# Transposes that read 104 of 128 partitions, loads by head padded to 48 rows, and new offsets in a planner's list

## The chip, the cores and the metric

The kernel runs on one core of one Trainium2 chip. The metric is the device time of one execution in microseconds (us). Three runs of the kernel before gave 744.09, 746.27 and 746.48 us, a median of 746.27. Inside the core, five engines work from queues of their own, each strictly in the order of its queue: TensorE (PE in the profile; its weight loads are shown apart as PEld), VectorE (DVE), ScalarE (ACT), GpSimd (POOL) and SyncE (SP). POOL and SP issue the DMAs here.

## What is computed

The kernel has two stages that follow one another. The first is a recurrence over 768 time steps for 4 batches x 8 heads with a 40 x 40 state each; the second is a two-layer network on the 3072 rows that the first stage gives:

```python
for t in range(S):                                   # S = 768, D = 40, 32 (batch, head) pairs
    y[:, :, t] = np.einsum('bhd,bhde->bhe', rt, state)
    Sa = np.einsum('bhde,bhe->bhd', state, at)
    state_decay = state * wt[:, :, None, :] - np.einsum('bhd,bhe->bhde', Sa, bt)
    state = state_decay + np.einsum('bhd,bhe->bhde', vt, kt)
...
h = x @ w_in                                         # 3072 x 320 times 320 x 2048
sp = np.where(h > 20.0, h, np.log1p(np.exp(np.minimum(h, 20.0))))
g = h * np.tanh(sp)
return (g @ w_out).astype(np.float32)                # times 2048 x 320
```

## The kernel before, in words

**Chunks.** The 768 steps are cut into 12 chunks (`c`) of 64 steps. Inside a chunk the recurrence is solved as a triangular system, so that it becomes matrix products. The 32 (batch, head) pairs are split three ways: `be` (two halves, for which most tiles exist twice), `al` (two halves that lie on partitions 0 to 39 and 64 to 103 of one tile; partitions 40 to 63 and 104 to 127 carry nothing), and 8 along the free dimension, which the steps take in two groups `g` of 4.

**Stages of a chunk.** `pre_a` (lines 316 to 413) prepares a chunk's half: loads `wa` (line 322) and `bk` (line 325), two scans on DVE (343, 348), products on PE (386) whose results ACT and DVE pick up (389 to 394), and transposes of `bk` on PE (410), copied by ACT (412). `inv` (415 to 479) inverts the 32 x 32 triangles of two chunks at once: a DVE transpose (420), then thirty rounds of a multiply (425) and an add (428), each of which needs the one before it, and two DVE transposes (430 into `TT`, 432 into `GP`). There are six such inverses. PE combines their results (444, 452) and forms `KT` (476). Then come the steps of the chunk, which carry the state `ST` from chunk to chunk: `step_a` (PE 514, ACT 517), `step_b` (PE 557, DVE 560), `step_u` (PE transposes 528, ACT 530), `step_d` (PE transposes 544 of the state, ACT 546 into `smd`), `step_c` (PE 586 and 591, DVE 596 and 602 make the new state, ACT 598 the output). `step_loads` (484 to 495) brings in the next chunk's `VS`, `UVT` and `bdr` from POOL's queue; `UVT` and `bdr` exist once, so the load of `bdr` for a chunk waits for the last line 591 of the chunk before it.

**The network.** Its weights are split into two parts of fewer bits by DVE and ACT (`convert`, lines 716 to 740: 12 pieces of `w_in` and 8 of `w_out`; DVE's part is lines 733, 734, 736 and 739). `load_x` (774 to 798) brings the recurrence's output back and splits it likewise (DVE 792, 794, 796; ACT 793). `mlp1` (PE 814, ACT 817 and 818, DVE 819) and `mlp2` (PE 835 to 837) make 48 units of work in a fixed chain.

**What sets the order.** No queue's order is written by hand. The code records its operations in a `Plan` with what each reads and writes, an estimated duration, and buffers drawn from pools; `Plan.order` (129 to 204) then places them one by one. Of the operations that could start on an engine within a look-ahead of the earliest, it takes the one with the highest priority: the length of the work that hangs on it plus an offset from `PRIO`, a table with one number for each kind of operation and chunk (`sa0` is `step_a` of group 0, and so on). The look-ahead is the constant `LOOK` plus an entry of the table `LOOKS`, which is empty before. So a change of these numbers, or of an operation's estimated duration, can move any instruction.

## Time and profile before

| what | before |
|---|---|
| median of three runs | 746.27 us |
| the profiled execution, its own time | 745.79 us |
| its span, first to last instruction | 744.0 us |
| PE busy / DVE busy / ACT busy / POOL busy | 678.6 / 456.0 / 420.8 / 102.2 us |
| first matmul of the network (line 814) starts | 393.74 us |
| moved by DMA | 61.81 MB, mean 83 GB/s |

Times inside the profile count from the span's start. A row of a table by line gives line, engine, operation, output and inputs, shapes, number of instructions, then the busy time, the mean duration of one in ns and the idle time in front of them with what ended it. In the chain of waits a row has start, duration and what stood there; in a table of stretches each engine has its busy time and, in brackets, the number of instructions, then come the granted TensorE clock, the DMA share and GB/s. A matmul in 32-bit floats counts as two instructions of PE, a transpose as one. The ends of matmuls are modelled, so that PE's busy time overstates how full it is; the pace of back-to-back matmuls (from the chain of waits) is the better measure.

### The profile page before, as it was taken

What the parts mean: (1) busy time and instruction counts of PE and PEld (TensorE: products, weight loads), DVE (VectorE), ACT (ScalarE), POOL (GpSimd) and SP (SyncE); (2) the same over time, 40 slices, a digit from 0 to 9 for tenths busy, and PEclk for the clock granted to TensorE, in tenths of its full rate; (3) what the DMA queues carried; (4) which work ended last, traced back from release to release, by engine and by line L of the source; (5) the groups of instructions that cost most, each with busy time, mean ns of one, the idle gap of its engine ahead of it and who ended that gap; (6) DMA issues with size and microseconds to landing.
All of it is one profiled execution on the core that took longest, in us unless ns stands there. A gap on an engine that the chain in (4) does not pass through costs nothing.

```text
span 744.0 us, 17243 instructions
## 1 busy us (share of the span) xinstructions
PE 678.6 (91%) x7048; PEld 626.0 (84%) x7048; DVE 456.0 (61%) x975; ACT 420.8 (57%) x937; POOL 102.2 (14%) x166
## 2 busy tenths in 40 slices
PE   2554698999999999999989999999999999999997
PEld 1544698998999989999978999898998989999897
DVE  7999999899999999999368853123113113111110
ACT  4554576867887787888858644234334324323332
POOL 9111013142224223212220000000000000000000
PEclk9778589999999999999999999999999999999999
DMA  7533214364444445144587713003004001000100
GB/s 191 171 98 89 64 39 104 77 139 116 107 109 111 101 118 150 37 117 128 123 220 185 206 46 100 0 12 97 14 1 103 18 1 40 19 0 1 36 1 35
DMA packets 58206, 61.81 MB, mean 83 GB/s; under 512 B 25536, under 2 KB 48704, under 8 KB 58128
## 3 DMA queue, kind: packets, MB, share of 16 engines
q1 hardware_dynamic: 49296, 40.94, 19.6%
q0 software_dynamic: 8832, 19.79, 10.8%
q8 instruction: 55, 0.90, 0.5%
q14 instruction: 23, 0.19, 0.1%
HBM read 48.79 MB, written 11.86 MB: 82 GB/s over the span
## 4 chain that ended last, share of the span: by engine, by line
PE 64%; DVE 22%; ACT 7%; issue 4%; DMA 1%; POOL 0%; ACTq 0%; DVEq 0%
PE ps L814 24%; PE ps L835 7%; PE ps L837 7%; PE ps L836 7%; PE ps L557 4%; DVE XL L428 3%; DVE tmp L425 3%; PE ps L386 3%; PE ps L586 3%; DVE P L343 2%; DVE bk L354 2%; PE ps L476 2%; PE ps L528 2%; DVE HA L394 2%; PE ps L591 1%
## 5 line engine op out<-in xcount | busy, mean ns | idle before, releaser
L819 DVE TENSOR_TENSOR gl<-g,gh 128x1024 fp32r<-128x1024 f32 x48 | 58.8, 1225 | 194.9 <-ACT gh L818 188.7
L817 ACT ACTIVATE g<-ps 128x512 f32<-128x512 f32 x96 | 57.0, 597 | 173.6 <-PE ps L814 173.3
L837 PE MATMUL ps<-w_oh,gl 128*128 128x320 f32 x384 | 118.6, 309 | 0.0
L835 PE MATMUL ps<-w_oh,gh 128*128 128x320 f32 x384 | 118.5, 309 | 0.0
L836 PE MATMUL ps<-w_ol,gh 128*128 128x320 f32 x384 | 118.5, 309 | 0.0
L814 PE MATMUL ps<-xh,w_ih 128*128 128x512 f32 x288 | 113.2, 393 | 0.0
L814 PE MATMUL ps<-xh,w_il 128*128 128x512 f32 x288 | 97.7, 393 | 0.0
L386 PE MATMUL ps<-bk,ad 128*128 128x168 f32 x384 | 68.7, 340 | 26.9 <-DVE bk L354 18.2
L386 PEld LDWEIGHTS ps<-bk,ad 128*128 128x128 f32 x384 | 63.8, 215 | 28.8 <-issue 26.5
L814 PE MATMUL ps<-xl,w_ih 128*128 128x512 f32 x192 | 75.4, 393 | 0.0
L836 PEld LDWEIGHTS ps<-w_ol,gh 128*128 128x128 f32 x384 | 72.1, 188 | 2.1
L835 PEld LDWEIGHTS ps<-w_oh,gh 128*128 128x128 f32 x384 | 72.1, 188 | 2.0
L837 PEld LDWEIGHTS ps<-w_oh,gl 128*128 128x128 f32 x384 | 72.1, 188 | 0.0
L814 PEld LDWEIGHTS ps<-xh,w_il 128*128 128x128 f32 x288 | 54.1, 188 | 12.3
L814 PEld LDWEIGHTS ps<-xh,w_ih 128*128 128x128 f32 x288 | 54.2, 188 | 10.6 <-issue 0.2
L428 DVE TENSOR_TENSOR XL<-XL,tmp 128x30 f32<-128x30 f32 (+9 forms) x180 | 58.7, 326 | 2.0
L425 DVE TENSOR_TENSOR tmp<-XL 128x30 f32<-128x30 f32 (+9 forms) x180 | 58.5, 325 | 1.7
L557 PE MATMUL ps<-bdr,UVT 128*128 128x128 f32 x384 | 48.8, 283 | 4.9 <-ACT UVT L517 2.7
L818 ACT CAST gh<-g 128x1024 fp32r<-128x1024 f32 x48 | 50.4, 1050 | 1.5
L557 PEld LDWEIGHTS ps<-bdr,UVT 128*128 128x128 f32 x384 | 46.1, 197 | 6.0 <-ACT UVT L517 3.4
L476 PE MATMUL ps<-bdT,HA 128*104 128x128 f32 x384 | 46.9, 280 | 2.4 <-ACT bdT L468 2.4
L476 PEld LDWEIGHTS ps<-bdT,HA 128*104 128x104 f32 x384 | 44.1, 174 | 4.1 <-ACT bdT L468 2.2
(89 smaller groups left out, 1170.9 us busy)
## 6 DMA issues: line engine op xcount, KB each, us to landing
wa<-in_wa SPq DMA_DIRECT2D x48, 162.5 KB
bk<-in_bk SPq DMA_DIRECT2D x48, 160.0 KB
cv<-in_wi SPq DMA_DIRECT2D x12, 512.0 KB
cv<-in_wo SPq DMA_DIRECT2D x8, 640.0 KB
pD<-P POOLq DMA_DIRECT2D x48, 81.2 KB, 2.5
bdr<-in_rD POOLq DMA_DIRECT2D x24, 160.0 KB, 4.5
UVT<-in_vD POOLq DMA_DIRECT2D x24, 160.0 KB, 4.0
VS<-in_vN POOLq DMA_DIRECT2D x24, 160.0 KB, 4.7
```

The lines of the kernel that those rows point to most:

```text
L386: PE.matmul(pv()[:, j], ad[:, s0 + j].rearrange("p k a t -> p (k a t)"), bk[:, s0 + j], start=(j == 0), stop=True, skip_group_check=True)
L425: op('V', (0.16 + m * i * 0.00104), lambda tv=tv, i=i, m=m: V.tensor_tensor(out=tv, in0=X[:, i + 1:32, i:i + 1].broadcast_to([128, m, i]), ...
L428: op('V', (0.16 + m * i * 0.00104), lambda tv=tv, i=i: V.tensor_tensor(out=X[:, i + 1:32, 0:i], in0=X[:, i + 1:32, 0:i], in1=tv, op=ALU.ad ...
L476: PE.matmul(kv()[:, j], ha.t[:, s0 + j], bd[:, o + s0 + j].rearrange("p a t -> p (a t)"), start=(j == 0), stop=True, skip_group_check=True)
L557: PE.matmul(qv()[:, s], UVT[:, g * 4 + s, be * 128:be * 128 + 128], bdr[:, be, g * 4 + s].rearrange("p a t -> p (a t)"), start=(s == 0), s ...
L814: PE.matmul(b.t, w, x, start=(n == 0), stop=(n == 7), skip_group_check=True)
L817: op('A', 0.6, lambda b=b, j=j: A.activation(g.t[:, j], b.t, AF.Mish), r=[b], w=[(g, j)])
L818: op('A', 1.05, lambda: A.copy(gh.t, g.t), r=[(g, 0), (g, 1)], w=[gh])
L819: op('V', 1.226, lambda: V.tensor_tensor(out=gl.t, in0=g.t, in1=gh.t.bitcast(F32), op=ALU.subtract), r=[(g, 0), (g, 1), gh], w=[gl])
L835: PE.matmul(o, gh.t[:, j, t], oh, start=(f == 0 and j == 0), stop=False, skip_group_check=True)
L836: PE.matmul(o, gh.t[:, j, t], ol, start=False, stop=False, skip_group_check=True)
L837: PE.matmul(o, gl.t[:, j, t], oh, start=False, stop=(f == 7 and j == 1), skip_group_check=True)
```

## The change

Four things are changed.

1. The three kinds of transposes on PE (lines 410, 528, 544) read partitions 0 to 103 of their input and multiply by a 104 x 104 part of the identity. So each gives 104 columns instead of 128, and four of them lie at a distance of 104 in PSUM. A helper `heads` picks the two times 40 wanted columns out of each. The copy of line 546 now takes only these 320 columns a partition (512 before), into an `smd` of 344 columns, and the matmul of line 591 takes its 64 weight columns from there at a distance of 40.
2. The loads of `wa`, `bk`, `UVT` and `bdr` bring 48 rows to each half's partitions instead of 40. The host pads the arrays with zeros (ones for the decay). So the partitions 40 to 47 and 104 to 111 are written by each load.
3. The planner's estimates for these operations are changed (for a group of four transposes 0.44 to 0.357, for the copy of line 546 0.58 to 0.43, lower figures for the loads).
4. `PRIO` has other numbers in every row, and `LOOKS` gets 21 rows.

```diff
+LOOKS = {
+    'zero': (0, 0, 0, 0, 0, 0.5, 0,),
...
 PRIO = {
-    'zero': (-99, -65, 338, 745, 81, -91, -72.5, 60, -47.5, -354, -210, 224.5,),
+    'zero': (-646.5, -1464.5, -1517.5, -811, -977, -824, -689, -662, -634.5, -1290, -1244, -1362,),
...
+    used = slice(0, 104)
+    rows = cst[used, 0:104]
+    heads = lambda x: bass.AP(x.tensor, x.offset, [x.ap[0], [104, 4], [64, 2], [1, 40]])
...
-    newSMD = make(wk, 2, [128, 4, 128], "smd")
+    newSMD = make(wk, 2, [128, 344], "smd")
...
+    op('G', 0.2, lambda: [G.memset(t[:, 320:344], 0.0) for t in S.smd], w=['smd0'])
...
-            q = slice(al * 64, al * 64 + 40)
-            op('S', 0.45, lambda q=q, al=al: SP.dma_start(out=wa[q], in_=I['wa'][c, be, al]), w=[('wz', be, al), ('a', be, al)], lat=1.95, srv=1.0)
+            q = slice(al * 64, al * 64 + 48)
+            op('S', 0.45, lambda q=q, al=al: SP.dma_start(out=wa[q], in_=I['wa'][c, be, al]), w=[('wz', be, al), ('a', be, al)], lat=1.95, srv=0.76)
...
-                    PE.transpose(pv()[:, j].rearrange("p a b -> p (a b)"), bk[:, s0 + j, xo:xo + 128], ident)
-            op('P', 0.44, tr, r=BK + ['cst', 'bkn0'], w=[b], mode=128, work=0.42, claim=[bkn])
+                    PE.transpose(pv()[:, j], bk[used, s0 + j, xo:xo + 128], rows)
+            op('P', 0.357, tr, r=BK + ['cst', 'bkn0'], w=[b], mode=128, work=0.347, claim=[bkn])
...
-                    PE.transpose(tv()[:, s].rearrange("p a d -> p (a d)"), UVT[:, g * 4 + s, be * 128:be * 128 + 128], ident)
+                    PE.transpose(tv()[:, s], UVT[used, g * 4 + s, be * 128:be * 128 + 128], rows)
...
-                PE.transpose(dv()[:, s], st[:, 2 * s:2 * s + 2].rearrange("p a d -> p (a d)"), ident)
-        op('P', 0.44, tr, r=[('ST', g), 'cst'], w=[b], mode=128, work=0.42)
-        op('A', 0.58, lambda: A.copy(smd.t, dv()), r=[b], w=[smd])
+                PE.transpose(dv()[:, s], st[used, 2 * s:2 * s + 2].rearrange("p a d -> p (a d)"), rows)
+        op('P', 0.357, tr, r=[('ST', g), 'cst'], w=[b], mode=128, work=0.347)
+        op('A', 0.43, lambda: A.copy(smd.t[:, 0:320].rearrange("p (s a d) -> p s a d", a=2, d=40), heads(b.t)), r=[b, 'smd0'], w=[smd])
...
-                            PE.matmul(py[be * 64:be * 64 + 64, 2 * j:2 * j + 2, 0:64], smd.t[:, s0 + j, be * 64:be * 64 + 64],
+                            PE.matmul(py[be * 64:be * 64 + 64, 2 * j:2 * j + 2, 0:64], smd.t[:, (s0 + j) * 80 + be * 40:(s0 + j) * 80 + be * 40 + 64],
```

The lines of the changed kernel are 28 higher than those of the kernel before, from the loads on. The number of matmuls, DVE and ACT operations and DMAs is the same; where they stand is not. Three places show it.

DVE, before, inside the sixth and last inverse (lines 425 and 428 are its rounds, 430 the transpose that ends them; 560, 596, 602 and 571 belong to the steps of a chunk, `cv` and `w_il` to the conversion of the network's weights):

```order
L739 SCALAR_TENSOR_TENSOR w_il_3855<-cv_3859,w_ih_3854 128x512
L425 TENSOR_TENSOR tmp<-XL 128x220
L596 TENSOR_TENSOR stn_135<-ST_115,ps_68 128x160
L428 TENSOR_TENSOR XL<-XL,tmp 128x11x20
L596 TENSOR_TENSOR stn_135<-ST_115,ps_63 128x160
L425 TENSOR_TENSOR tmp<-XL 128x210
L602 TENSOR_TENSOR ST_115<-stn_135,R_134 128x8x40
L428 TENSOR_TENSOR XL<-XL,tmp 128x10x21
L596 TENSOR_TENSOR stn_136<-ST_116,ps_65 128x160
L425 TENSOR_TENSOR tmp<-XL 128x198
L571 TENSOR_TENSOR R_134<-rw_130,rw_131 128x8
L428 TENSOR_TENSOR XL<-XL,tmp 128x9x22
```

DVE, changed, from the end of the same inverse (458 is 430 before, 624 is 596, 630 is 602, 599 is 571, 762 and 767 are 734 and 739):

```order
L458 STREAM_TRANSPOSE TT<-XL 128x32x32
L624 TENSOR_TENSOR stn_135<-ST_115,ps_66 128x160
L460 STREAM_TRANSPOSE GP_149<-TT 64x32x32
L624 TENSOR_TENSOR stn_135<-ST_115,ps_69 128x160
L624 TENSOR_TENSOR stn_136<-ST_116,ps_63 128x160
L630 TENSOR_TENSOR ST_115<-stn_135,R_133 128x8x40
L624 TENSOR_TENSOR stn_136<-ST_116,ps_64 128x160
L599 TENSOR_TENSOR R_133<-rw_130,rw_131 128x8
L630 TENSOR_TENSOR ST_116<-stn_136,R_134 128x8x40
L599 TENSOR_TENSOR R_134<-rw_130,rw_131 128x8
L762 SCALAR_TENSOR_TENSOR cv_3983<-cv_3983 128x512
L767 SCALAR_TENSOR_TENSOR w_il_3977<-cv_73,w_ih_3976 128x512
```

The state update of one chunk (two of line 602 with what leads to them) and part of the weights' conversion stood ahead of the end of the inverse and stand behind it now. Counted over the whole queue ahead of the sixth line 430: four of line 596, two each of 571, 602, 733, 734 and 736 and three of 739 fewer than before. A round of the inverse (425 or 428) that follows another with nothing between them is found 108 times in the six inverses before, and 80 times in the changed queue (31 and 43 of these in the sixth).

PE, before, ahead of the first use of the sixth inverse (line 444 reads `TT`; 528 and 557 are transposes and products of the ninth chunk, counted from 0):

```order
L528 MATMUL ps_67<-cst,UVT 128x128 x4
L557 MATMUL ps_68<-bdr,UVT 128x128 x4
L557 MATMUL ps_63<-bdr,UVT 128x128 x4
L528 MATMUL ps_64<-cst,UVT 128x128 x4
L528 MATMUL ps_65<-cst,UVT 128x128 x4
L444 MATMUL ps_66<-TT,GP_149 32x32 x32
```

PE, changed, behind the first use of the sixth inverse (472 is 444 before, 542 is 514, 572 is 544, 556 is 528, 585 is 557):

```order
L472 MATMUL ps_65<-TT,GP_149 32x32 x32
L542 MATMUL ps_62<-KT_127,VS_109 64x64 x8
L542 MATMUL ps_62<-KT_128,VS_110 64x64 x8
L542 MATMUL ps_66<-KT_127,VS_109 64x64 x8
L542 MATMUL ps_66<-KT_128,VS_110 64x64 x8
L572 MATMUL ps_69<-cst,ST_116 128x104 x4
L556 MATMUL ps_67<-cst,UVT 128x104 x4
L556 MATMUL ps_62<-cst,UVT 128x104 x4
L556 MATMUL ps_66<-cst,UVT 128x104 x4
L556 MATMUL ps_68<-cst,UVT 128x104 x4
L585 MATMUL ps_67<-bdr,UVT 128x128 x4
L585 MATMUL ps_66<-bdr,UVT 128x128 x4
```

The ninth chunk's products, which stood ahead of that use, stand behind it. Counted from the first line 444 of the sixth inverse to the end of the recurrence, PE has 16 transposes of line 528, 8 of line 544, 16 products of line 557, 32 of line 514, 8 of line 586 and 4 of line 591 more than before.

DVE, changed, behind the last product of the recurrence that it picks up (588 is 560 before; 820, 822 and 824 are 792, 794 and 796, which prepare the first input of the network; 761, 762 and 764 are 733, 734 and 736):

```order
L588 TENSOR_TENSOR UVQ_113<-ps_68,cst 128x8x64
L762 SCALAR_TENSOR_TENSOR cv_73<-cv_73 128x640
L820 TENSOR_TENSOR xy_4591<-xy_4591,xp_4592 128x768
L764 SCALAR_TENSOR_TENSOR cv_73<-cv_73 128x640
L761 TENSOR_SCALAR cv_3983<-cv_3983 128x512
L822 TENSOR_TENSOR xl_4594<-xy_4591,xh_4593 128x2x256
L824 TENSOR_TENSOR xh_4593<-xy_4591,xh_4593 64x256
```

Before, line 792 stood ahead of the last two of line 560, and a row of 733, 794, 734 and 796 behind them. The order of PE inside the network is as before.

More of the change, by code (lines that the diff above doesn't have):

```diff
@@ L224, in layouts @@
     wt = w.transpose(4, 2, 1, 6, 3, 0, 5).reshape(nch, 2, 2, 40, 8, C)
[L225 to L227 removed]
+    wa = np.zeros((nch, 2, 2, 48, 1040), np.float32)
+    wa[..., 40:, :520].reshape(nch, 2, 2, 8, 8, 65)[..., 1:] = 1
+    wa[..., :40, :520].reshape(nch, 2, 2, 40, 8, 65)[..., 1:] = wt
+    wa[..., :40, 528:] = a.transpose(4, 2, 1, 6, 3, 0, 5).reshape(nch, 2, 2, 40, 512)
     o['wa'] = wa
@@ L523, in step_u @@
                 b = newPS()
-                tv = lambda b=b: view(b, full, 512, "p (s a d) -> p s a d", s=4, a=2)
+                tv = lambda b=b: view(b, full, 416, "p (s x) -> p s x", s=4)
                 def tr(be=be, tv=tv):
                     for s in range(4):
-                        PE.transpose(tv()[:, s].rearrange("p a d -> p (a d)"), UVT[:, g * 4 + s, be * 128:be * 128 + 128], ident)
-                op('P', 0.44, tr, r=UV(g) + ['cst'], w=[b], mode=128, work=0.42)
-                op('A', 0.43, lambda be=be, tv=tv: A.copy(UVQ[be][:, g * 8:g * 8 + 8, 64:104], tv()[:, :, :, 0:40].rearrange("p s a d -> p (s a) d")),
+                        PE.transpose(tv()[:, s], UVT[used, g * 4 + s, be * 128:be * 128 + 128], rows)
+                op('P', 0.357, tr, r=UV(g) + ['cst'], w=[b], mode=128, work=0.347)
+                op('A', 0.43, lambda be=be, b=b: A.copy(UVQ[be][:, g * 8:g * 8 + 8, 64:104].rearrange("p (s a) d -> p s a d", a=2), heads(b.t)),
                    r=[b], w=[('U', be, g)])
```

32 lines of the change are left out of this document (15 added, 17 removed), and 74 rows, old and new, of tables (LOOKS, PRIO).

## The prediction

> **What bounds the kernel now.** I read the busy shares first, then a table of stretches cut where the work changes, then the chain of waits and the order of time at the seams. The profiled execution took 745.79 us (span 744.0), 0.5 under the median of 746.27; the sum is made against 745.79. About 0.3% (2.2 us) is what a measurement of this kernel can tell from no change.
>
> ```profile
> PE 678.6 (91%) x7048; PEld 626.0 (84%) x7048; DVE 456.0 (61%) x975; ACT 420.8 (57%) x937; POOL 102.2 (14%) x166
> ...
> 90.00:345.00 255.00, 245.31 (x3980) 231.07 (x3976) 242.29 (x621) 203.08 (x535) 66.07 (x102) 0.98 0.40 106
> 345.00:394.00 49.00, 44.78 (x851) 42.24 (x851) 29.23 (x56) 36.71 (x81) 9.78 (x14) 0.97 0.58 147
> 394.00:739.00 345.00, 345.00 (x1914) 312.09 (x1914) 101.44 (x111) 135.58 (x194) 1.01 (x2) 1.00 0.17 46
> ```
>
> The 91% of the page hide two limits. From 394 to 739 us the network runs and PE is busy for all of 345.00 us. The change leaves its instructions and their order alone, so these 345 us stay. From 90 to 345 us two engines are nearly full: DVE is busy for 242.29 of 255 us, and PE for 245.31, which is overstated since its ends are modelled. DVE is the one that I take as the bound there: what ends that stretch is the sixth inverse, a chain on DVE, and the steps of two chunks hang on it. From 345 to 394 DVE has only 29.23 us of work and PE sets the pace. So two questions decide: how early DVE ends the sixth inverse, and how much PE has left then.
>
> ```profile
> 338.11 0.70 DVE L734 SCALAR_TENSOR_TENSOR cv<-cv 128x512 int32<-128x512 int32 x1
> 338.72 0.29 DVE L425 TENSOR_TENSOR tmp<-XL 128x130 f32<-128x130 f32 x1
> 338.93 0.69 DVE L736 SCALAR_TENSOR_TENSOR cv<-cv 128x512 int32<-128x512 int32 x1
> ...
> 341.71 0.22 DVE L425 TENSOR_TENSOR tmp<-XL 128x58 f32<-128x58 f32 x1
> 341.97 0.22 DVE L428 TENSOR_TENSOR XL<-XL,tmp 128x58 f32<-128x58 f32 x1
> ...
> 342.68 2.01 DVE L430 STREAM_TRANSPOSE TT<-XL 128x1024 f32<-128x1024 f32 x1
> ```
>
> **The change, part by part.**
>
> *DVE ahead of the end of the sixth inverse.* That end is the transpose of line 430, 342.68 + 2.01 = 344.69 us. The rows show how a round costs less where other work stands between: line 425 starts at 338.72, 0.09 before line 734 has ended (338.11 + 0.70 = 338.81), and line 736 starts 0.08 before 425 has ended. Where a round follows a round, line 428 starts at 341.97, 0.04 after the end of 425 (341.93), because it needs its result. So an instruction between rounds takes 0.08 less than its duration, and a bare pair of rounds 0.04 + 0.08 = 0.12 more than a filled one. The order has 80 such bare pairs where there were 108: 28 x 0.12 = 3.4 us less. And these no longer stand ahead of the end:
>
> ```profile
> L571 DVE TENSOR_TENSOR R<-rw,rw 128x8 f32<-128x8 f32 x22 | 3.4, 159 | 0.0
> L596 DVE TENSOR_TENSOR stn<-ST,ps 128x160 f32<-128x160 f32 x44 | 13.8, 315 | 3.7 <-ACT yev L598 1.6 <-PE ps L591 1.5 <-PE ps L586 0.2
> L602 DVE TENSOR_TENSOR ST<-stn,R 128x320 f32<-128x320 f32 x22 | 10.6, 482 | 0.0
> L733 DVE TENSOR_SCALAR cv<-cv 128x512 int32<-128x512 int32 x12 | 5.5, 457 | 3.5 <-DMA cv<-in_wi 3.5
> L734 DVE SCALAR_TENSOR_TENSOR cv<-cv 128x512 int32<-128x512 int32 x12 | 8.3, 688 | 12.0 <-ACT cv L732 11.9
> L736 DVE SCALAR_TENSOR_TENSOR cv<-cv 128x512 int32<-128x512 int32 x12 | 8.2, 688 | 0.1
> L739 DVE SCALAR_TENSOR_TENSOR w_il<-cv,w_ih 128x512 fp32r<-128x512 f32 x12 | 8.1, 678 | 1.8 <-ACT w_ih L738 1.8
> ```
>
> Two of 571, four of 596, two of 602, two each of 733, 734 and 736, three of 739: 0.32 + 1.26 + 0.96 + 0.91 + 1.38 + 1.38 + 2.03 = 8.2 us, less 17 x 0.08 for the overlap: 6.9. Together with 3.4 the inverse ends 10.3 us earlier, if DVE waits as long as before.
>
> *DVE's waits* are the unknown. Of its 255 - 242.29 = 12.7 idle us in that stretch some 101 bare pairs x 0.04 = 4.0 are the chain itself; 8.7 are waits, on ACT and PE mostly. PE has less to do ahead of this point (below), ACT a little less. All 8.7 could go, or as much could be added; I take 1.0 less, near no change, since no row tells which of them go.
>
> *The transposes.* Their pace is read from the chain of waits:
>
> ```profile
> 119.74 1.79 PE ps L557 x16
> ...
> 203.63 0.44 PE ps L544 x4
> ...
> 204.94 0.86 PE ps L586 x16
> 205.81 0.44 PE ps L591 x8
> ...
> 209.32 1.08 PE ps L514 x32
> 210.40 0.24 PE ps L368 x8
> ...
> 211.66 0.87 PE ps L528 x8
> ...
> 216.09 1.75 PE ps L476 x16
> ...
> 220.84 0.29 PE ps L386 x2
> ```
>
> Eight transposes of line 528 take 0.87 us, 109 ns each, with 128 weight columns and 128 moving columns. Line 476 has 104 weight columns and 128 moving ones and takes 1.75 / 16 = 109 as well; line 386 has 128 weight columns and 168 moving ones and takes 145. So the pace goes with the moving columns, (145 - 109) / 40 = 0.9 ns for each, and 104 instead of 128 of them save 20 to 22 ns; I take 20. Could the weight load hold the pace instead? Line 368 has 64 weight columns and 16 moving ones: 0.24 / 8 = 30 ns each, which makes 60 ns for 128 columns, under the 89 that would be left.
>
> The Trainium skill speaks against that: by its page "TensorE: Matmul & The Clock Gate", section "LDWEIGHTS (loading the stationary operand)", a weight load's time goes with its columns (columns / 1.2 in ns) and not with its rows. By that, an estimate of 107 ns for 128 columns, a transpose would stay at 109 ns and the sum would be the third rival's below; the 30 ns of line 368 are less than the 53 that the rule gives for 64 columns.
>
> ```profile
> L410 PE MATMUL ps<-cst,bk 128*128 128x128 f32 x192 | 25.4, 282 | 2.4 <-ACT ad L352 2.4
> L528 PE MATMUL ps<-cst,UVT 128*128 128x128 f32 x176 | 22.8, 275 | 1.0 <-ACT UVT L517 1.0
> L544 PE MATMUL ps<-cst,ST 128*128 128x128 f32 x88 | 13.6, 279 | 1.1 <-DVE ST L602 1.1
> ```
>
> 192 + 176 + 88 = 456 transposes save 9.1 us of PE. But only 56 of them stand behind the first use of the sixth inverse (32 of line 528, 24 of line 544, where PE sets the pace): 1.1 us count. The other 400, 8.0 us, lie beside DVE's chain and are worth nothing, as long as DVE is the bound there.
>
> *PE behind the end of the inverse* gets more to do. By the paces above: 16 of line 528 1.74, 8 of 544 0.88, 16 products (32 instructions) of 557 3.58, 32 products of 514 (64 instructions) 2.16, 8 of 586 0.86, 4 of 591 0.44: 9.6 us, of which the 1.1 are saved again.
>
> ```profile
> 346.90 1.20 PE L444 MATMUL ps<-TT,GP 32*32 32x32 f32 x64
> ...
> 377.50 0.61 PE L591 MATMUL ps<-bdr,smd 128*64 128x128 f32 x8
> ...
> 380.40 2.08 PE L514 MATMUL ps<-KT,VS 104*64 104x64 f32 x64
> 384.73 5.32 PE L557 MATMUL ps<-bdr,UVT 128*128 128x128 f32 x32 [2.24 <-DMA bdr<-in_rD]
> ```
>
> Before, PE began with line 444 at 346.90, 2.2 us after 344.69, since it was busy with the ninth chunk's products, which now stand behind. With 17.6 us less ahead of it (9.6 moved, 8.0 saved) PE will stand at 472 and wait, and begin 0.2 after the end: 2.0 less.
>
> *The load of `bdr` for the last chunk* starts after the last line 591 of the chunk before (377.50) and holds line 557 until 384.73.
>
> ```profile
> 379.29 1.69 POOL L494 DMA_DIRECT2D bdr<-in_rD  x2 [4.13 <-issue]
> ...
> 388.90 0.95 DVE L792 TENSOR_TENSOR xy<-xy,xp 128x768 f32<-128x768 f32 x1
> ...
> 392.61 0.42 DVE L796 TENSOR_TENSOR xh<-xy,xh 64x256 fp32r<-64x256 f32 x1
> ...
> 393.74 0.50 PE L814 MATMUL ps<-xh,w_ih 128*128 128x512 f32 x1
> ```
>
> In these 7 us PE had two groups of 544 and two of 514 to do; the order leaves it one of the former fewer (0.44), and 48 rows instead of 40 change the issue (1.69 for two) and the landing by at most a fifth of 5.4 us, up or down. Between -1.1 and +1.5 I take 0.4 more. Behind 792, 794 and 796 stands the network's first matmul (393.74, 0.7 after 796 ended). Now 792 (0.95) comes behind the last 560, with one more conversion: about 1.4 later less the 0.7 of slack, 0.7 more; between 0 and 1.5.
>
> *What is hidden.* The copy of line 546 falls from 512 to 320 columns, which cost 436 ns at line 412; 22 x 0.15 = 3.4 us of ACT, which is busy for 203.08 of 255 us and does not end the chain. The loads of `wa` and `bk` bring a fifth more bytes; DVE waits for no such load in that stretch, since each is issued many microseconds ahead. The small memset on POOL lies at its start. If a load did come late, it would show as one of DVE's waits above.
>
> ```profile
> L412 ACT COPY bkn<-ps 128x320 f32<-128x320 f32 x48 | 18.9, 436 | 5.3 <-PE ps L410 5.1
> L546 ACT COPY smd<-ps 128x512 f32<-128x512 f32 x22 | 12.9, 589 | 0.4 <-PE ps L544 0.2
> ```
>
> **The sum:** -10.3 (DVE to the end of the inverse) - 1.0 (waits) + 9.6 - 1.1 (PE behind it) - 2.0 (PE already there) + 0.4 (`bdr`) + 0.7 (first input of the network) = -3.7. 745.8 - 3.7 = **742.1 us**.
>
> **Rivals.**
>
> *First: PE is the bound from 90 to 345 us.* For it speaks 245.31 of 255 us; against it that what DVE did there ended the stretch, and that PE's pace sums to less than its modelled busy time. Then all 9.1 us of PE's saving count: 745.8 - 9.1 + 0.4 + 0.7 = 737.8.
>
> *Second, slower: more foreign work inside the rounds holds the chain.* DVE takes its queue strictly in order. Filling 28 more pairs saves 0.12 each only if the filler's input is there; if it is not, the next round waits behind it.
>
> ```profile
> DVE HA L394 <- ACT GP L391: 3.6, 9, 0.8
> ```
>
> Such a wait took 3.6 / 9 = 0.4 before. If all 28 wait that long, 28 x 0.4 = 11.2 us come on top and the 1.0 falls away: 742.1 + 12.2 = 754.3. It is slower than before once 12 of the 28 wait. Against it: DVE waited for only 8.7 us in all with 252 fillers.
>
> *Third: the transposes are not faster*, since something else than the moving columns sets their 109 ns. Then only 1.1 us is lost, 743.2, because the rest is hidden anyway.
>
> **How the numbers follow.** The forecast gets 0.52, the first rival 0.15, the second 0.16, the third 0.17. The forecast's own range is 738 to 746, from the waits and the two last terms. The whole range, 737 to 749, takes in the first and third rival and the nearer half of the second. Faster by over 0.3%: 0.36 of the forecast's 0.52, all of the first rival, 0.10 of the third: 0.61. Within 0.3%: 0.13 + 0.04 + 0.06 = 0.23. Slower: 0.03 + 0.12 + 0.01 = 0.16.
>
> **What would show it.** The sixth line 458 (430 before) ends at 333 to 335 us, and line 472 starts within 0.3 us of it. DVE's idle time up to there is near 12 us; 20 or more speaks for the second rival. Eight transposes take 0.71 us; 0.87 is the third rival. The first matmul of the network starts near 390 us, and 345 us follow. I am wrong if the end of the inverse moves by 10 us and the network does not start earlier, or if PE is already late at line 472: then PE was the bound.

## The result: slower by 0.8%, and the profile after

| | before | after |
|---|---|---|
| median (8 runs each, taken together) | 746.38 us (744.09 to 747.80) | 753.06 us (749.25 to 754.14) |
| the profiled execution, its own time | 745.79 us | 754.14 us |
| its span | 744.0 us | 752.4 us |
| sixth inverse ends (line 430, now 458) | 344.7 us | 342.7 us |
| from there to the network's first matmul | 49.1 us | 59.2 us |

The ratio of the times is 1.008, with a 95% interval of 1.0056 to 1.0104. The forecast was 742.1 us and its range ended at 749, so the forecast missed, and with the wrong sign. Against the sum of the prediction, the profiled execution lost 9.3 us in front of the end of the sixth inverse (11.3 earlier foreseen, 2.0 found) and 2.5 behind it (7.6 longer foreseen, 10.1 found). The network takes what it took: from its first matmul to its last 346.4 us before and 346.6 after.

The stretches of the kernel after, with the columns of the prediction's table:

```profile
90.00:345.00 255.00, 238.42 (x3882) 224.74 (x3884) 235.20 (x612) 193.79 (x523) 57.42 (x96) 0.96 0.48 106
345.00:394.00 49.00, 42.66 (x779) 39.57 (x774) 23.82 (x47) 36.32 (x81) 12.56 (x20) 0.99 0.66 150
```

DVE is idle for 255 - 235.20 = 19.8 us from 90 to 345 us, where it was 12.7 before. What it waited for in that stretch (us in total, times, longest):

```profile
DVE bk L382 <- DMA bk<-in_bk: 7.9, 5, 2.8
DVE HA L422 <- ACT GP L419: 3.6, 9, 0.7
```

The first row is new: before, DVE waited for no load in that stretch. The chain of waits of the kernel after shows how such a wait comes about (start, duration, what stood there):

```profile
149.78 1.24 PE ps L438 x12
...
151.34 6.97 DMA bk<-in_bk
...
158.43 1.23 DVE bk L382
...
175.33 1.08 PE ps L438 x12
176.69 7.82 DMA bk<-in_bk
184.63 1.24 DVE bk L382
```

The transposes of line 438 are the last readers of the old `bk`. The new order puts them late, the load of the next `bk` cannot be issued before they are done, and it then takes 7 to 8 us. DVE comes to line 382 before the load has landed. A table of stretches (PE, PEld, DVE, ACT and POOL busy, the granted clock, the DMA share, GB/s) shows two things more:

```profile
151.00:158.40 7.40, 7.40 (x96) 7.04 (x94) 4.25 (x12) 6.55 (x17) 0.93 (x2) 1.00 0.98 148
176.70:184.60 7.90, 5.97 (x101) 5.23 (x100) 5.59 (x19) 5.83 (x14) 3.23 (x6) 1.00 1.11 209
184.60:190.00 5.40, 4.04 (x14) 4.07 (x15) 4.14 (x7) 1.01 (x4) 0.00 (x0) 0.52 0.62 139
```

While these loads are under way the 16 DMA engines are full (0.98 and 1.11); at the like places before, from the issue of the load to line 354, the share was 0.63 and 0.72. And PE, which stands idle for 1.15 and then 2.14 us around the second wait, has a granted clock of 0.52 over the 5.4 us that follow: its 16 instructions of line 414 take 4.82 us, 301 ns each, where the prediction read 145. So the loss goes on after the wait; that the idle time brings the lower clock is what the order of events suggests, no run here tests it.

Behind the sixth inverse, the rest of the chain of waits of the kernel after:

```profile
346.58 5.37 DMA bdr<-in_rD
...
352.08 2.02 PE ps L585 x16
...
364.01 1.15 PE ps L480 x64
...
365.65 0.52 POOL UVT L519
...
368.83 0.73 POOL bdr L522
...
369.65 0.94 POOL yD L651 x2
...
370.72 5.65 DMA bdr<-in_rD
...
376.51 3.82 PE ps L585 x32
...
387.03 5.54 DMA bdr<-in_rD
...
392.71 5.44 PE ps L585 x32
```

Three times the chain goes through a load of `bdr`, for chunks 9, 10 and 11 (counted from 0), the last two with other issues of POOL in front. Before, it went through such a load once, for the last chunk. PE is far from idle meanwhile, as the stretch from the end of the inverse to the network's first matmul shows:

```profile
342.70:401.80 59.10, 52.76 (x984) 49.20 (x980) 33.25 (x64) 41.79 (x92) 12.56 (x20) 0.97 0.63 151
```

PE is busy for 52.8 of 59.2 us, where it was busy for 44.8 of 49.0; its waits for `bdr` grew from 2.2 to 5.2 us. So the moved work and the loads lie side by side here. To see why the loads are late, take POOL's rows in order of time, the kernel before first:

```profile
354.44 1.69 POOL L494 DMA_DIRECT2D bdr<-in_rD  x2 [5.67 <-PE ps L591]
356.12 1.08 POOL L623 DMA_DIRECT2D yD<-yev  x2
```

and after:

```profile
365.65 1.31 POOL L519 DMA_DIRECT2D UVT<-in_vD  x2 [11.83 <-PE ps L480]
368.83 0.73 POOL L522 DMA_DIRECT2D bdr<-in_rD  x1 [1.87 <-PE ps L619]
369.65 1.08 POOL L651 DMA_DIRECT2D yD<-yev  x2
370.72 0.76 POOL L522 DMA_DIRECT2D bdr<-in_rD  x1
```

These are the loads for chunk 10. They wait for chunk 9's last readers. Before, those were done at 354 us, and PE could begin chunk 10 only at 365.25 (line 514), when `KT` was ready: the load lay in that hole. In the new order chunk 9's last products stand inside chunk 10's step, as PE's order of time shows, before and after:

```profile
365.25 2.08 PE L514 MATMUL ps<-KT,VS 104*64 104x64 f32 x64
367.77 3.84 PE L557 MATMUL ps<-bdr,UVT 128*128 128x128 f32 x32 [0.43 <-ACT UVT L517]
```

```profile
365.07 1.15 PE L542 MATMUL ps<-KT,VS 104*64 104x64 f32 x32
...
367.20 0.88 PE L614 MATMUL ps<-UVQ,bkn 128*64 128x104 f32 x16
367.92 0.61 PE L619 MATMUL ps<-bdr,smd 128*64 128x128 f32 x8
...
376.51 0.68 PE L585 MATMUL ps<-bdr,UVT 128*128 128x128 f32 x4 [0.16 <-DMA bdr<-in_rD]
```

Both kernels begin chunk 10's step at 365 us. Its products with `bdr` follow 2.5 us later before, 11.4 us later after. From line 514 (542) of chunk 10 to that of chunk 11 it is 15.15 us before and 20.76 after. But the last row also says that PE waited only 0.16 us for that load: it had work of its own, 10.4 us of it, nearly up to the moment when the load landed. Of the 10.1 us by which the way from the inverse to the network is longer, 1.8 lie ahead of chunk 10's step, 5.6 in it and 2.7 behind it.

### The profile page after: what moved, and what is told of

The parts are those of the page before. It is cut to its first block, busy times and chain, and to the rows that moved or that the text cites. A ratio compares the mean times of both kernels' runs of the same rounds, so it can differ in the third digit from the quotient of the medians.

```text
span 752.4 us, 17245 instructions
## 1 busy us (share of the span) xinstructions
PE 676.4 (90%) x7048; PEld 623.9 (83%) x7048; DVE 454.6 (60%) x975; ACT 416.8 (55%) x937; POOL 96.2 (13%) x168
## 3 DMA queue, kind: packets, MB, share of 16 engines
q0 software_dynamic: 8064, 21.31, 12.1%
## 4 chain that ended last, share of the span: by engine, by line
PE 67%; DVE 13%; DMA 8%; issue 6%; ACT 5%; POOL 1%; SPq 0%; DVEq 0%; ACTq 0%; POOLq 0%
PE ps L842 24%; PE ps L863 7%; PE ps L865 7%; PE ps L864 7%; PE ps L414 5%; PE ps L585 4%; PE ps L614 4%; DMA bdr<-in_rD 3%; DMA bk<-in_bk 3%; DVE XL L456 2%; PE ps L504 2%; DVE tmp L453 2%; PE ps L619 2%; DVE bk L382 2%; DVE P L371 1%
## 5 line engine op out<-in xcount | busy, mean ns | idle before, releaser
L414 PE MATMUL ps<-bk,ad 128*128 128x168 f32 x384 | 72.5, 353 | 45.6 <-DVE bk L382 27.2
L414 PEld LDWEIGHTS ps<-bk,ad 128*128 128x128 f32 x384 | 67.5, 225 | 47.7 <-issue 40.1
L842 PEld LDWEIGHTS ps<-xh,w_ih 128*128 128x128 f32 x288 | 54.2, 188 | 10.6 <-ACT yev L626 0.2
L585 PEld LDWEIGHTS ps<-bdr,UVT 128*128 128x128 f32 x384 | 46.9, 200 | 10.1 <-ACT xh L821 4.2
L504 PE MATMUL ps<-bdT,HA 128*104 128x128 f32 x384 | 48.5, 283 | 3.2 <-ACT bdT L496 3.2
L504 PEld LDWEIGHTS ps<-bdT,HA 128*104 128x104 f32 x384 | 44.8, 176 | 4.8 <-ACT bdT L496 3.5
```

The costliest lines, as they stand in the source:

```text
L414: PE.matmul(pv()[:, j], ad[:, s0 + j].rearrange("p k a t -> p (k a t)"), bk[:, s0 + j], start=(j == 0), stop=True, skip_group_check=True)
L504: PE.matmul(kv()[:, j], ha.t[:, s0 + j], bd[:, o + s0 + j].rearrange("p a t -> p (a t)"), start=(j == 0), stop=True, skip_group_check=True)
L585: PE.matmul(qv()[:, s], UVT[:, g * 4 + s, be * 128:be * 128 + 128], bdr[:, be, g * 4 + s].rearrange("p a t -> p (a t)"), start=(s == 0), s ...
L842: PE.matmul(b.t, w, x, start=(n == 0), stop=(n == 7), skip_group_check=True)
```

## The experiments

Each kernel is timed against the kernel before on the same chip. Every queue keeps the order of the kernel that the edit starts from, apart from rows that the edit itself takes out or adds, save for the three kernels with mixed tables. A profile is one execution, and executions of one kernel lie 2 to 12 us apart, so times are compared by the ratio; from the profiles I take what repeats in many. In the table "front" is the time from the end of the first line 458 to the end of the sixth, "tail" from there to the network's first matmul, "step" from line 542 of chunk 10 to that of chunk 11 (line 514 in the order of before).

| kernel | median us | ratio, 95% | front | tail | step |
|---|---|---|---|---|---|
| before | | 1 | 256.8 | 49.1 | 15.1 |
| after | 753.06 | 1.0080 (1.0056 to 1.0104) | 256.8 | 59.2 | 20.8 |
| old_order_104 | 744.53 | 0.9970 (0.9958 to 0.9982) | 259.5 | 48.9 | 14.9 |
| old_order_48rows | 749.94 | 1.0041 (1.0025 to 1.0057) | 258.5 | 48.4 | 15.2 |
| new_order_alone | 755.60 | 1.0116 (1.0096 to 1.0137) | 253.4 | 64.0 | 26.3 |
| new_order_40rows | 757.14 | 1.0133 (1.0101 to 1.0164) | 251.4 | 62.7 | 24.6 |
| new_order_two_bk | 750.33 | 1.0055 (1.0035 to 1.0076) | 257.5 | 58.7 | 21.3 |
| new_order_two_bdr | 751.62 | 1.0057 (1.0030 to 1.0083) | 250.4 | 60.1 | 21.1 |
| old_order_104_two_bdr | 745.89 | 0.9989 (0.9969 to 1.0009) | 257.5 | 47.1 | 14.8 |
| new_order_few_weights | 753.04 | 1.0088 (1.0058 to 1.0119) | 256.0 | 58.3 | 21.8 |
| old_order_few_weights | 747.71 | 1.0020 (0.9994 to 1.0046) | 260.6 | 47.8 | 15.2 |
| new_order_two_bk_few_weights | 751.44 | 1.0053 (1.0028 to 1.0077) | 251.9 | 56.7 | 20.4 |
| new_order_half_kt | 751.41 | 1.0057 (1.0036 to 1.0079) | 252.7 | 60.7 | 22.8 |
| old_order_half_kt | 747.64 | 1.0014 (0.9999 to 1.0028) | 260.2 | 49.2 | 15.8 |
| new_then_old | 772.78 | 1.0342 (1.0319 to 1.0365) | 273.4 | 54.4 | 14.2 |
| new_then_old_two_bk | 774.41 | 1.0374 (1.0340 to 1.0409) | 278.4 | 55.0 | 14.4 |
| new_then_old_40rows | 770.98 | 1.0318 (1.0292 to 1.0344) | 277.5 | 54.5 | 14.8 |
| new_order_two_bdr_half_kt | 751.31 | 1.0046 (1.0018 to 1.0074) | 251.9 | 56.8 | 20.9 |
| new_order_all_three | 748.35 | 1.0018 (0.9988 to 1.0047) | 251.3 | 56.5 | 20.8 |
| old_order_two_bdr_half_kt | 747.08 | 0.9995 (0.9969 to 1.0022) | 257.7 | 48.0 | 17.8 |

### Which part of the change

Four kernels separate the order from the transposes and from the 48 rows. They were built from after by taking edits back, or from before by making some, with the planner's numbers left alone so that the order stays. The copies behind the transposes follow them in `old_order_104`; line 546's copy is of 320 columns both there and, since it was left as in after, in `new_order_alone`:

```diff
 new_order_40rows, against after (the same for bk, UVT and bdr):
-            q = slice(al * 64, al * 64 + 48)
+            q = slice(al * 64, al * 64 + 40)
 new_order_alone: this and, for the three transposes,
-                    PE.transpose(pv()[:, j], bk[used, s0 + j, xo:xo + 128], rows)
+                    PE.transpose(pv()[:, j], bk[:, s0 + j, xo:xo + 128], ident)
 old_order_104, against before:
-                    PE.transpose(pv()[:, j].rearrange("p a b -> p (a b)"), bk[:, s0 + j, xo:xo + 128], ident)
+                    PE.transpose(pv()[:, j], bk[used, s0 + j, xo:xo + 128], rows)
 old_order_48rows, against before:
-            q = slice(al * 64, al * 64 + 40)
+            q = slice(al * 64, al * 64 + 48)
```

> The changed kernel with its order kept instruction for instruction; only the loads of wa, bk, UVT and bdr bring 40 rows again. Theory R (the 48 rows cost it: in the changed profile a 512-byte packet of bk takes 47 ns instead of 31 and DVE waits 7.9 us for bk between 90 and 345 us): most of the 7 to 8 us lost against the kernel before come back, 743 to 747 us, and DVE's wait for bk falls under 2 us. Theory O (the order alone: it starts the loads of bk too close to their use): 750 to 753 us, and DVE still waits 5 us or more for bk.

> The new order with the transposes of 128 partitions and the loads of 40 rows of before: the order by itself. Theory R: 744 to 748 us. Theory O: 750 to 756 us. If the transposes' saving lies beside DVE's chain, it is 1 to 2 us above new_order_40rows; if PE is the bound, up to 9 us above it.

> The kernel before with its order kept and the transposes of 104 partitions alone. If DVE is the bound from 90 to 345 us, only the transposes where PE sets the pace count (32 behind the end of the sixth inverse, 0.7 us) and what PE no longer holds up: 743 to 746 us. If PE is the bound: about 737 us.

> The kernel before with its order kept and loads of 48 rows alone. Theory R: 3 to 8 us slower than before, 749 to 754 us, with waits of DVE for bk. Theory O: within 2 us of before, because that order starts the loads early enough.

Measured: the order alone costs 1.2%, the transposes alone bring 0.3%, the 48 rows alone cost 0.4%. So the loss is the order's. `new_order_40rows`, at 757.14 us, lies outside what both theories named, with 4.3 us of waits for `bk`. Its transposes of 104 partitions bring nothing in the new order that the runs can tell (1.0133, and 1.0116 with 128). In the old order the 48 rows cost 0.4% without any wait of DVE for `bk` from 90 to 345 us, so Theory R's mechanism is not what is seen there, and why they cost stays open. In the new order the loss is smaller with the 48 rows than without (1.0080 against 1.0133, from runs made apart, with intervals that just meet), which was not expected; the chain of waits of `new_order_40rows` shows a part of why, at the same place as above:

```profile
365.19 7.80 DMA bdr<-in_rD
...
373.13 5.45 PE ps L585 x32
```

There, with other loads under way, a `bdr` half of 40 rows takes 7.80 us where 48 rows took 5.65, and PE's granted clock behind the longer wait is 0.72 from 373 to 379 us (5.45 us for what takes 3.82). At this place the half takes 7.8 and 8.2 us in the two profiles with 40 rows and 5.2 to 6.7 in the eight with 48.

### The waits for `bk`, and a second `bdr`

A second tile takes away what a load waits for. For `bk` there was room for one more tile, so `be=0` got it, for which the three long waits were:

```diff
-    bkb = tiles(cp, 2, [128, 8, 168], "bk")
+    bkb = tiles(cp, 3, [128, 8, 168], "bk")
-        wa, bk, ad = wab[be], bkb[be], adb[be]
+        wa, bk, ad = wab[be], bkb[be if be else c % 2 * 2], adb[be]
 two_bdr:
-    bdr = cs.tile([128, 2, 8, 2, 64], F32, name="bdr")
+    bdrs = tiles(cs, 2, [128, 2, 8, 2, 64], "bdr")
-            op('G', 0.85, lambda q=q, al=al: G.dma_start(out=bdr[q, :, :, al].rearrange(
+            op('G', 0.85, lambda q=q, al=al: G.dma_start(out=bdrs[c % 2][q, :, :, al].rearrange(
```

> The kernel of after with a second bk tile for be=0, used by odd chunks; every engine's order stays. In the profile of after, VectorE waits 7.9 us for bk loads between 90 and 345 us, and the three long waits (158.4, 184.6, 299.5 us) are all for be=0. Theory L (the new order brings the use of bk too close behind its load, and this is what eats the gain in front of the sixth inverse): these waits go, line 458 ends at 335 to 337 instead of 342.7, the tail behind it stays near 59 us, and the time is 746 to 748, 1.000 of the kernel before. Rival T (the tail is paced by its own bdr loads and steps, so an earlier line 458 is lost there): line 458 ends early, the tail grows as much, 751 to 754. Rival W (the 16 DMA engines are full there, so the wait only goes to the next load, wa or bk of be=1): line 458 stays at 341 to 343, 752 to 754.

> The kernel of after with two bdr tiles, used by even and odd chunks; every engine's order stays. In the profile of after, TensorE waits 0.94, 0.16 and 4.10 us for bdr behind the sixth inverse, and the group of line 585 that follows the longest wait takes 5.44 us instead of 3.8. Theory D (the single bdr tile sets the tail of the new order): these waits and the slow group go, the tail from line 458 to the network is 52 to 53 us instead of 59.1, the time 746 to 748. Rival M (the PE work that the new order puts behind the sixth inverse sets the tail, the load only fills a hole in it): the tail shrinks by 1.5 at most, 751 to 753. Rival C (a bdr load that is issued earlier collides with the bk loads on the DMA engines): VectorE's waits for bk grow over 7.9 us and the time is 753 or more.

> The order of before with the transposes of 104 partitions and two bdr tiles, loads of 40 rows. In the profile of the same kernel with one bdr tile, TensorE waits 2.88 us for bdr at 387.0 and the group behind it takes 5.38 us instead of 3.84. Theory D: both go, 744.5 becomes 740 to 741, 0.992 of the kernel before. Rival M (KT, VS or the output of the chunk before is as late): 743 to 745.

With the second `bk` the waits for it fell from 7.9 to 0.6 us. The ratio went from 1.0080 to 1.0055, some 2 us; the intervals overlap, and they do for two kernels further down that differ by the same tile and ran together (1.0088 and 1.0053). The profiled execution even ended line 458 at 343.3, because others took their place:

```profile
DVE stn L624 <- PE ps L619: 5.8, 4, 5.0
```

Five of these 5.8 us are one wait, of a filler between two rounds of an inverse:

```profile
203.03 0.32 DVE L624 TENSOR_TENSOR stn<-ST,ps 128x160 f32<-128x160 f32 x1 [5.03 <-PE ps L619]
```

So Theory L is right about the waits and wrong about their price: of 7.9 us some 2 come back, as an estimate from the ratios.

The second `bdr` tile did not shorten the step (21.1 us), and the time, 751.62, is what rival M had named. POOL's rows of that kernel tell why:

```profile
363.01 0.73 POOL L522 DMA_DIRECT2D bdr<-in_rD  x1
365.72 1.08 POOL L651 DMA_DIRECT2D yD<-yev  x2 [1.97 <-ACT yev L626]
366.79 0.76 POOL L522 DMA_DIRECT2D bdr<-in_rD  x1
```

The first half no longer waits for chunk 9's readers, but between the halves stands the store of chunk 9's output, which waits for chunk 9's last products, and POOL issues in order. So the second half starts where it started without the tile: 366.79 is 5.65 us behind the start of line 542 (361.13 in that profile), and in the kernel after it is 370.72 - 365.07 = 5.65. And at the last chunk another wait took over, as the chain of waits of the same kernel shows:

```profile
381.07 9.06 DMA cv<-in_wo
...
390.15 0.50 DVE cv L761
```

DVE stood at a conversion whose load was late, and the product that it should have picked up (588) stood behind it in DVE's queue. In the old order the second tile halved TensorE's last wait (2.88 to 1.21 us), but the time is 0.9989 of before against 0.9970 without it: no gain that the runs can tell.

### Emptier DMA engines

The engines are 0.88 to 1.09 busy from 370 to 395 us, and loads of the network's weights of 512 and 640 KB are part of that. So the loads of `w_out` and of the last quarter of `w_in` were cut to one partition (two small loads at first use fill the buffers, and the shift of line 764 is by 0 for these pieces):

```diff
+            r = slice(0, 1) if key[0] == 'wo' or key[1] == 3 else slice(0, 128)
-                SP.dma_start(out=b.t[:, 0:n].rearrange("p a b -> p (a b)"), in_=src.bitcast(I32))
+                SP.dma_start(out=b.t[r, 0:n].rearrange("p a b -> p (a b)"), in_=src[r].bitcast(I32))
```

> The kernel of after, in which the loads of the second weight matrix and of the last quarter of the first bring one partition instead of 128 (5 KB instead of 640, 4 instead of 512); their conversions run on what the buffer holds, so the network's output is left wrong. Every instruction keeps its place. Behind the sixth inverse the 16 DMA engines are 0.88 to 1.09 busy from 370 to 395 us in the profile of after, and there the weight loads and the bdr, UVT and VS loads share them. Theory Q (the last bdr load is late because the DMA engines are full): the tail from line 458 to the network shrinks from 59.1 to 54 to 56 us, TensorE's 4.10 us wait for bdr at 392.71 goes under 2, the time is 748 to 750. Rival M (the tail is set by the PE work put there and by steps that wait on each other; the bdr load waits for its readers, not for engines): the tail stays at 58 to 60, 751 to 754.

> The same cut of the weight loads in the kernel of before, as a control. In the profile of before the DMA engines are 0.80 to 0.96 busy from 370 to 385 us and TensorE waits 2.24 us for bdr at 384.73. Theory Q: the tail shrinks by 1 to 2 us, from 49.0 to 47 or 48, 744.5 to 746. If it gains as much as the new order does (3 to 5), the full engines are no cost of the new order. Rival M: no change, 746 to 747.5.

> The new order with both remedies: the second bk tile for be=0, and the weight loads of one partition (the network's output is left wrong by them). Theory L and Q together (the new order loses by its loads alone, at two places): 745 to 747, level with the kernel before, line 458 at 335 to 339 and a tail of 54 to 56 us. Rival M (the work moved behind the sixth inverse costs what the time in front of it gains): 749 to 751, as with the second bk tile alone.

Neither order gained (1.0088, 1.0020), and the step stayed at 21.8 us. From 370 to 395 us the engines are 0.67 busy instead of 0.97. Theory Q's price falls: the last half of `bdr` takes 4.7 us instead of 5.5, and PE still waits 3.2 us ahead of the line 585 that reads it. For chunk 10's load the test is not clean, since from 375 to 380 us the engines are still 0.89 busy, and its second half takes 6.69 us. Together with the second `bk` the ratio is 1.0053, what the second `bk` gave alone.

### Less work for PE

Does PE's own work behind the sixth inverse set the end, as the prediction had it? Half of one group of matmuls was left out for the last two chunks:

```diff
-                        for j in range(4):
+                        for j in range(2 if last else 4):        # last: the sixth inverse
                             PE.matmul(kv()[:, j], ha.t[:, s0 + j], bd[:, o + s0 + j].rearrange("p a t -> p (a t)"), start=(j == 0),
```

> The kernel of after, in which line 504 issues two of its four matmuls for the last two chunks (the other half of their KT is stale, so the last two chunks come out wrong). That takes 32 of 64 matmuls of 117 ns (3.74 us by 32), 3.7 us of TensorE work, out of the stretch behind the sixth inverse, and nothing else. Theory M (behind the sixth inverse TensorE's own work sets the end, 52.8 us busy of 59.1 in the profile of after): the tail shrinks by 3 to 4 us, the time is 749 to 750, 1.003 to 1.004 of the kernel before. Rival S (there the loads of bdr and UVT and the steps that wait on one another set the end): it shrinks by 1 at most, 752 to 753.

> The same half of line 476 left out in the kernel of before (44.8 us busy of 49.0 behind the sixth inverse). Theory M: 742.5 to 743.5, 0.995 of the kernel before. Rival S: 745.5 to 746.5.

3.7 us of PE's work less, and the tail is 60.7 us in the new order and 49.2 in the old. In the new order the waits for loads grew in its place:

```profile
372.66 5.19 PE L585 MATMUL ps<-bdr,UVT 128*128 128x128 f32 x32 [2.37 <-DMA bdr<-in_rD]
```

Up to this line PE had 8.6 us of work in the step instead of 10.4, and yet the line starts 12.1 us into the step instead of 11.4, since the second half of `bdr` landed no earlier. In the whole tail PE's busy time fell by 0.8 us only (52.8 to 52.0), with a granted clock of 0.92 instead of 0.97. The time of the new order came down a little (1.0057, between what the two theories named), with intervals that overlap. So PE's work alone does not set the end, as Theory M had it: where it is shortened, the loads hold the end in its place. That PE's work is no limit at all does not follow.

### The old table for the last three chunks

The tables of after with before's numbers for chunks 9 to 11 give an order whose PE rows behind the sixth inverse follow the old sequence, while the first 537 rows of DVE are those of after:

```diff
-    'sa0': (-229.5, 278, 162, -85.5, 446.5, 72.5, 540, 578.5, 307.5, 234.5, 163, 274.5,),
+    'sa0': (-229.5, 278, 162, -85.5, 446.5, 72.5, 540, 578.5, 307.5, 926.5, 790, 831,),
...
```

> The kernel of after with the table columns of chunks 9 to 11 from before; VectorE's order is the one of after for its first 537 rows, and behind the sixth inverse TensorE's order is before's again: both halves of KT for the last pair first, then chunk 10's step without anything of chunk 9 or of KT inside it. VectorE has 801 rows in front of the last transpose of line 458's group (792 in after, 807 in before). Theory O2 (of the order's loss, the larger part lies in the tail, where chunk 10's step takes 20 to 22 us from its line 542 to the next chunk's, against 15 in the order of before): the tail is 48 to 51 us instead of 57 to 64, chunk 10's step 15 to 16, line 458 ends at 340 to 345, the time is 744 to 747, 0.997 to 1.001. Rival M2 (the tail only holds the time that the front gave up; what comes back into the front is paid there): line 458 ends at 348 or later, 750 to 753. Rival R (the padded rows or the smaller transposes make the tail long in any order): tail 57 or more.

> The kernel before this one in the list with the second bk tile for be=0. Theory L (the waits for bk in the front cost their length, 5 to 8 us in the profiles of the new order): 2 to 4 us less than without, 741 to 744. Rival T (the front's waits cost little at the end, as the second tile gave the new order 2 us of 7.9): within 1.5 us of the one without.

> The first kernel of the list with loads of 40 rows, order unchanged. In the old order 48 rows cost 0.4%, in the new one they gained 0.5%. If 48 rows cost in themselves (each packet takes longer, 47 against 31 ns by 512 B): 2 to 3 us less than with 48. If the order of the tail decided that, too (the bdr load on its chain): within 1.5 us.

Chunk 10's step is 14.2 to 14.8 us in all three, as in the old order, and the tail 54.4 to 55.0. But the sixth inverse ends only at 362 to 364 us, so the whole is 3% slower, which none of the theories had named; mixing two tables spoils the front by more than the tail gains, and the network takes 348 to 351 us. The tail is still some 6 us longer than in the old order, and PE waits 4.5 to 5.8 us for `bdr` in it. It does show that the step's length follows the sequence: 20 to 26 us in the ten profiles of the new order, 14 to 16 in these three and in six of the seven of the old (17.8 in one). The second `bk` tile brings nothing here (1.0374 against 1.0342), and 40 rows are 0.24% better than 48, with intervals that overlap.

### Two and three at once

> The kernel of after with two bdr tiles and, in addition, half of line 504 left out for the last two chunks (these come out wrong). Each of the two edits alone left chunk 10's step at 20 to 23 us. Theory B (two things of about the same length lie on that step, the bdr load that starts behind chunk 9's last reader, and the PE rows of chunk 9 and of KT that stand in front of line 585; taking one away leaves the other): chunk 10's step, from its line 542 to the next chunk's, is 16 to 18 us, the tail 54 to 56, the time 747 to 749, 1.001 to 1.003. Rival N (neither is on it): the step stays at 20 or more, 750 to 752.

> The same, and the weight loads of one partition as well (the network's output is left wrong), so that the DMA engines have room when the bdr loads run. Theory B with the DMA engines as a third part: another 1 to 3 us less than with two edits, the tail 51 to 54 us, 745 to 747. Rival N: as with two edits, within 1 us.

> The control: the order of before with the transposes of 104 partitions, two bdr tiles and half of the KT matmuls (line 476 of before) left out for the last two chunks. There chunk 10's step has neither in it (15 us). Theory B: as with two bdr tiles alone, 744 to 746, 0.997 to 0.999. If both edits shorten any order alike (rival A): 3 to 5 us less, 741 to 742.

The edits are those above. The step stays at 20.9 and 20.8 us where Theory B named 16 to 18; the control in the old order gains nothing either (0.9995). With all three edits the time is level with before (1.0018), by a tail of 56.5 and a short front. The chain of waits of `new_order_all_three` says what holds line 585 there:

```profile
359.05 1.08 PE ps L542 x32
...
361.29 0.71 PE ps L614 x16
362.00 0.46 PE ps L619 x8
362.55 0.33 DVE stn L624
362.91 0.38 ACT yev L626
...
363.57 0.94 POOL yD L651 x2
364.64 5.68 DMA bdr<-in_rD
370.45 3.81 PE ps L585 x32
```

Here the path is whole in one view: chunk 9's last products (614, 619), their eviction (626), the store on POOL's queue (651), behind it the second half of `bdr`, 5.68 us of landing, and line 585. From line 542 to the issue of that half it is 5.65 to 5.68 us in every one of the ten profiles of the new order, whatever the edit: 370.72 - 365.07 = 5.65 after, 364.64 - 358.98 = 5.66 here (PE's order of time has line 542 at 358.98; the chain counts it from 359.05). No edit that was tried touches this sequence, so no run took the late load away, and Theory B is not decided.

The other of its two things is there as well. Between line 542 and line 585 PE has 10.2 to 10.6 us of work of its own in the seven profiles with all of `KT` (8.6 in the three with half), and line 585 starts 11.0 to 14.0 us in. In two of the seven, with the second `bdr` tile and with the second `bk` and few weights, PE came to line 585 after the load had landed. In `new_order_two_bdr` the load landed at 372.74, and the chain of waits goes through PE's rows:

```profile
372.57 0.36 PE ps L572 x4
372.93 3.75 PE ps L585 x32
```

So the late load and the rows that stand in front of line 585 take about the same time, and taking one away leaves the other. The edit that would bring the load forward, the store moved behind both halves of it, was not run. In the kernel after, PE waited only 0.16 us for that load, so by itself it could hardly shorten this step; with half of `KT` left out as well it could save, as an estimate, up to the 1.6 to 2.4 us that PE waits there.

## Why the prediction was wrong

**"DVE waits for no such load in that stretch, since each is issued many microseconds ahead."** This step failed, and with it the condition of the term of -10.3 us ("if DVE waits as long as before") and the -1.0 for the waits. Most of the work left as counted: in the front DVE is busy for 237.2 us instead of 244.1. But it is idle for 19.6 us instead of 12.7, 7.9 of them for `bk`, and nothing is left of the gain. The sentence is true of the order of before; a new order also moves the last readers of `bk` (line 438) and so the moment from which its load can be issued.

One pair of profiles overstates this. The profiled execution of after is the longest of its eight. Over the ten profiles of the new order (those with mixed tables left out) the front is 250.4 to 257.5 us, mean 253.3, over the seven of the old order 256.8 to 260.6, mean 258.7. So the order does bring the sixth inverse forward by some 5 us, half of the 11.3 that were counted; in the pair above it is 0.0, the start of the front being 2.1 earlier. In the means DVE is busy for 236.9 us instead of 244.2, 7.4 less where the sum had 9.1 (6.9 and 28 x 0.08), and idle for 16.5 instead of 14.4, where the sum had 2.1 less. The waits for `bk`, 4.2 us in the mean and none in the old order, more than make this up; those for PE and ACT are 9.1 us in both. What they cost at the end is some 2 us by `new_order_two_bk`, with others in their place. Three of the ten fronts are over 255 us, and they are the three with the lowest granted clock (0.94 to 0.95; 0.96 to 0.98 in the other seven). Whether the low clock makes them long, or the waits that go with it, is not shown.

**"PE sets the pace" from 345 to 394 us.** This step failed in part. 7.6 us were summed there, most of it 9.6 of PE's moved work, and 10.1 came. PE's busy time did grow by 8.0, about as the moved work lets expect; its waits for `bdr` grew by 3.0, where the sum had 0.4. Wrong is that PE alone sets the pace. In the kernel before, the chain of waits from 354.5 to 367.7 us already runs over ACT, with 1.14 us of PE between, through the copies of `KT` for example:

```profile
364.49 2.04 ACT KT L479 x4
```

And in the new order, with 3.7 us of PE's work left out, the loads hold the end. What was missed is that a moved step takes its loads along. I priced the `bdr` load of the last chunk (0.4 more; its landing went from 4.46 to 5.54 us) and not that of chunk 10, which before was hidden in the 11 us until `KT` was ready, nor that of chunk 9. With chunk 9's last products behind the start of chunk 10's step, the store and the load came beside PE's own rows: line 585 starts 8.9 us later within the step, and the step itself is 5.6 us longer. Which of the two would give way first stays open.

**The transposes** had their pace sized rightly. Eight of line 556 in the chain of waits of the kernel after:

```profile
333.62 0.71 PE ps L556 x8
```

0.71 us is what the prediction named as the sign, 89 ns each. The third rival falls. By the Trainium skill ("TensorE: Matmul & The Clock Gate", section "LDWEIGHTS (loading the stationary operand)") a load of 128 weight columns takes 128 / 1.2 ns, and so, as an estimate, would have held the pace at 107 ns; the trace disagrees. By themselves, with the narrower copy, they gave 0.3% in the old order, 1.3 to 3.1 us by the interval, where 1.1 was counted, and nothing that the runs can tell in the new one.

**The 48 rows** were costed at nearly nothing. The issue of a half of `bk` became a fifth shorter (764 to 608 ns), that of `bdr` a seventh, but alone they cost 0.41% in the old order (in the mixed one 0.24%, with intervals that overlap), and where the `bdr` load is on the path they seem to help. So their sign seems to hang on the order, and one term for them, worked out from one place, was too little.

**Nearly as foreseen:** line 472 starts 0.37 us behind the end of the sixth inverse (0.3 was named; 0.05 to 0.46 in the other nine profiles). But PE did not stand and wait there: it was busy with line 619 until then. The network takes what it took.

**The first rival** falls for the old order: with PE as the bound `old_order_104` would have taken about 737 us, and it took 744.5.

**The second rival** named the right sign, DVE idle for 20 us or more (19.8), in the kernel after for another reason: not fillers in the rounds, but a load. Its own mechanism is seen where the waits for `bk` are gone: with the second `bk` tile a filler between two rounds (line 624) waits 5.0 us for PE, and in the kernel that has few weights too 3.8. At the last chunk, with two `bdr` tiles, foreign work holds DVE's queue as well (line 761 waiting for `in_wo`).

## What to carry to other kernels

When an order changes, redo for each load three times: when its last reader is done, what stands ahead of its issue on the issuing queue (a store of the chunk before is enough), and when it is needed; a load hidden in a hole is free only as long as the hole stays between its last reader and its use. A stretch in which an engine looks full need not be set by that engine: leave a few microseconds of its work out and see whether the end moves, and if it does not, what holds it then. And of a change with several parts the good one may be worth keeping alone: here the smaller transposes in the old order, 0.997 (0.9958 to 0.9982), beat both kernels by a little; with a second `bdr` tile added, 0.9989, a gain can no longer be told.

## What the hardware showed unexpectedly

A load of 48 partitions uses more DMA engines than one of 40, and is hardly faster for it. The trace has 3,216 four-byte packets on the queue of `wa` and `bk` before and 3,792 after, 6 more for each of the 96 loads. By the Trainium skill ("DMA: Bandwidth & Descriptors", section "Why a DMA increments its semaphore by 16 and not by 1") each engine that takes part posts one write to the semaphore, and the number of engines is the largest up to 16 that divides the slowest dimension of both sides, here the partitions: 10 for 40, 16 for 48. The trace agrees. But a 512-byte packet takes 43 ns instead of 31 on average in the old order, with 48 and with 40 rows, and 47 instead of 33 in the new. From issue to the last packet a `bk` load takes 3.8 us in the median where it took 4.0 in the old order, and 4.5 with both in the new. The queue's rows of before and of `old_order_48rows`, which has the same order:

```profile
q1 hardware_dynamic: 49296, 40.94, 19.6%
```

```profile
q1 hardware_dynamic: 53328, 44.11, 24.8%
```

8% more bytes take 27% more of the engines' time (24.8% of a span of 746.6 us against 19.6% of 744.0).
